# Warm-up products, key products in column tiles, a later exponential and finer transfers in a linear-attention and expert kernel

## The chip, the cores and the metric

The kernel runs on one core of a Trainium2 chip. The metric is the device time of one execution in microseconds (us). A core has TensorE (PE, with its weight loads shown apart as PEld), VectorE (DVE), ScalarE (ACT), GpSimd (POOL) and SyncE (SP, which here issues nearly all transfers). They run on their own instruction queues, each in order, and meet through semaphores.

## The reference

Two stages, in float32. Attention: 4 batches, 8 heads, 576 tokens, width 64. A feature map projects q and k by one 64x128 matrix, subtracts the largest absolute value of each row, and takes the exponential of both signs:

```python
proj = np.einsum('bhsd,df->bhsf', x, w_phi)
proj = proj - np.max(np.abs(proj), axis=-1, keepdims=True)
return np.concatenate([np.exp(proj), np.exp(-proj)], axis=-1)
...
kv = np.einsum('bhsf,bhsd->bhfd', k_p, v);  z = np.sum(k_p, axis=2)
num = np.einsum('bhsf,bhfd->bhsd', q_p, kv)
den = np.einsum('bhsf,bhf->bhs', q_p, z)[..., None] + 1e-06
```

Then a mixture of 8 experts over the 2304 tokens (512 wide): argmax of the gate's logits picks one expert, each expert takes the first 576 tokens that chose it, and computes `relu(x @ w1) @ w2` (512 to 1024 to 512), scaled by the gate's weight.

## The kernel before

The tokens are taken in two halves of 1152 (p = 0, 1), each of 9 blocks of 128 rows; heads go in two groups of four (g = 0, 1). An item is one block of one head group: 18 key items, then 18 query items for each half, 72 in all. A loop over t (L673) issues the items as a software pipeline: in step t stand the projection of item t, the maximum and subtraction of item t-1 (`center`, L263), the exponentials or transposes of item t-2, the products with kv of query item t-3, and the sums of key item t-4 (`kv_sum`, L328). The order of instructions on each engine is the order in which this loop writes them.

- **Projection** (`project`, L246). The first seven key blocks multiply raw float32 columns (L254). All others use a float16 split: `x_split` (L189) makes on ACT the rounded half and on POOL the remainder (L194, L195), and eight products of 128x128 by the two float16 parts of the matrix follow (L259, L260).
- **Sums of keys** (L342). Each item has 16 products of 64 columns of weights, alternating between the lower and the upper half of the output partitions, each as two passes.
- **Gates.** `vgate` puts the gate's logits of the values beside them (L219, L229, L241).
- **Routes.** `route` (L415) queues small steps for a group of blocks in `pending`; `tick()` works them off in between DVE's instructions of `center`. For the first group (9 blocks) ACT takes the exponential `es` right after the one-hot rows `oh` (L481), then DVE reduces `oh` (L536), then `swaps` finds the fullest expert and POOL reorders the experts (L488 to L496), and `sel` reads the reordered offsets `perm["s"]` (L539). The logits `lt` that `es` reads and the results of L536 lie in one PSUM tile, `sm_t`.
- **Transfers.** All wait in SP's queue. `paced` lets a transfer wait for the latest subtraction of `center`. Empty rows are written to `xs` by 18 fills of 256 rows (L157), paced, at t from 18 to 47. `x_load` (L180) brings a tile of q or k whole, not paced, eight steps ahead of its split; the second half's `v` and `vT` come in four transfers at t = 19 and 23. Scatters of rows (L459) begin at t = 56.

`warm` (L278) issues products of the identity into the PSUM tile `pt`; nothing calls it. After the attention the experts' products follow (L814 to L848), weights loaded per expert.

Of the kernel before, what the change touches and what calls it, by code (L numbers as in the profile page):

```python
# [20 lines left out]
P = 128  # L21
# [11 lines left out]
XW = DM + 2  # L33
# [4 lines left out]
def tile_kernel(ctx: ExitStack, tc: tile.TileContext, qT, kT, vT, vv, w_phi, w_g, w1, w2, out, cap):  # L38
# [110 lines left out]
    def paced(dma):  # L149
        tc.add_manual_dep(dma.ins, beat[0].ins.name, mybir.DependencyInfo(  # L150
            mybir.DependencyClass.Sync, mybir.DependencyReason.DATA), reason="pace")

    def fill_xs(i, n):
        r0, r1 = (NE * slots * j // n for j in (i, i + 1))
        nr = (r1 - r0) // P
        if nr:
            paced(nc.sync.dma_start(xs[r0:r0 + nr * P, :].rearrange("(r p) c -> p r c", p=P),  # L157
                                    fill.unsqueeze(1).to_broadcast([P, nr, XW])))
        if r1 - r0 - nr * P:
            nc.sync.dma_start(xs[r0 + nr * P:r1, :], fill[0:r1 - r0 - nr * P])  # L160

    tokf = cpool.tile([P, NT // P], F32, tag="tokf", name="tokf")
    nc.gpsimd.iota(tokf, pattern=[[P, NT // P]], base=SKIP, channel_multiplier=1,
# [16 lines left out]
    def x_load(kind, p, g, c, cut=0):  # L180
        c0, c1 = runs[c]
        if (kind, p, g, c) not in raw_x:
            raw_x[kind, p, g, c] = px_p.tile([P, 2, c1 - c0], F32, tag=f"px{c}", name="px")
        lo, hi = (0, cut) if cut > 0 else (-cut, c1 - c0)
        src = (kT if kind == "k" else qT)[2 * g:2 * g + 2, :, p * TP + c0 + lo:p * TP + c0 + hi]
        nc.sync.dma_start(raw_x[kind, p, g, c][:, :, lo:hi], src.rearrange("i d c -> d i c"))


    def x_split(kind, p, g, c, odd):  # L189
# [58 lines left out]
    def project(kind, p, g, r):  # L248
        pr = ps_p.tile([P, 4, NF], F32, tag="pr", name="pr")
        c = int(r > MIX)  # L250
        cols = slice(r * P - runs[c][0], (r + 1) * P - runs[c][0])
        if (kind, p, g) == ("k", 0, 0) and r < 7:
            for i in range(2):
                nc.tensor.matmul(pr[:, 2 * i:2 * i + 2], raw_x[kind, p, g, c][:, i, cols], wpair,  # L254
                                 start=True, stop=True)
        else:
            for j in range(4):
                lt = stk[kind, p, g, c, j % 2][:, j // 2, cols]
                nc.tensor.matmul(pr[:, j], lt, whi, start=True, stop=False)  # L259
                nc.tensor.matmul(pr[:, j], lt, wlo, start=False, stop=True)  # L260
        return pr

    def center(pr):  # L263
# [151 lines left out]
    def route(blk, n, xr, lg):  # L415
# [106 lines left out]
        def ready():  # L522
# [9 lines left out]
            lambda: v.scalar_tensor_tensor(ef, lt, 0.0, io, ALU.is_ge, ALU.mult),  # L532
            lambda: v.tensor_reduce(flat(ix), ef, AX.X, ALU.min),
            lambda: v.tensor_tensor(oh, ix.to_broadcast([P, n, NE]), io, ALU.is_equal),
            *([number, exps] if late else [exps] if old is None else []),
            lambda: v.tensor_reduce(rn[:, 0], oh.rearrange("p n e -> p e n"), AX.X, ALU.add),  # L536
            run_total,
            *([*swaps(), rest, rest, rest] if old is None else []),
            lambda: v.tensor_tensor(sel, oh, perm["s"].unsqueeze(1).to_broadcast([P, n, NE]), ALU.mult),  # L539
            lambda: v.tensor_reduce(flat(sl), sel, AX.X, ALU.add),  # L540
            positions,
            *([] if late or old is None else [exps, rest, rest, rest]),
# [77 lines left out]
    def attention():  # L620
# [4 lines left out]
        def plan(c, marks):  # L625
            ends = []
            for x, split in zip([(K, 0, 0)][:c] + [(K, 0, 1), (Q, 0, 0), (Q, 0, 1), (K, 1, 0), (K, 1, 1), (Q, 1, 0), (Q, 1, 1)], marks):
                for odd in range(2):
                    at.setdefault(split[odd], []).append((*x, c, odd))
                ends.append(max(split))  # L630
                if x[:2] != (K, 0):
                    free = ends[-4] if len(ends) > 3 else 6
                    load_at.setdefault(max(free + 2, min(split) - 8), []).append((*x, c))

        plan(0, [(5, 6), (12, 13), (15, 16), (25, 26), (31, 32), (42, 44), (46, 49)])
        plan(1, [(3, 4), (10, 11), (19, 21), (23, 24), (28, 29), (37, 39), (55, 51), (57, 53)])
# [11 lines left out]
        x_load(K, 0, 1, 1)  # L648
        v_load(0, MIX + 1, NBLK, 1)
        rests = []  # L650

        def bank(i):
            def f():
# [8 lines left out]
            for i, f in enumerate(parts):  # L662
                early.setdefault(t + min(i, 3 - t) if t == 2 else t + i, []).append(f)

        FILLS = [*range(18, 36, 3), *range(36, 48)]
        OPEN = 56
        depth = 4
        for t in range(len(items) + depth):
            for i, lag in ((0, 0), (2, 2), (3, 3), (6, 4), (1, 1), (4, 4), (7, 5)):
                n = t - lag  # L670
                if 0 <= n < len(items) and items[n].get(i):
                    items[n][i]()
            for f in early.get(t, []):  # L673
                f()
            for f in rests:
                f()
            calm[0] = 0 if t < 36 or len(swapped) > 1 else 2 if t in (46, 49) else 1
            for x in load_at.get(t, []):
                x_load(*x)
            rests = [x_split(*x) for x in at.get(t, [])]  # L680
            if scatters and t >= OPEN:
                scatters.popleft()()
            if t >= len(items):
                for _ in range(4):
                    if pending:
                        step()
            if t in FILLS:
                for i in range(len(FILLS)):
                    if FILLS[i] == t:
                        fill_xs(i, len(FILLS))  # L690
            if t in (19, 23):
                vt_load(1, 0, NBLK, (t - 19) // 4)
                v_load(1, 0, NBLK, (t - 19) // 4)
            if t == 54:
                assert swapped
                for e in range(NE):
                    who[e] = nc.values_load(perm_i[0:1, e:e + 1], engines=[mybir.EngineType.SP], min_val=0,
                                            max_val=NE - 1)
            if 56 <= t < 72 and t % 2 == 0:
                half = (t - 56) // 2  # L700
                paced(w_load(0, half // 2, half % 2 * 2, half % 2 * 2 + 2))
            if t == 60:
                rctx.close()
                first_p.append(ctx.enter_context(tc.tile_pool(name="first_p", bufs=1, side="right")))
                for c in range(2):
                    w_t[c] = w_pair(first_p[0], c)
                x2_l.append(first_p[0].tile([P, 4, 2, slots], F32R, tag="xh", name="xh"))
                for s0, _ in tiles[:2]:
                    xi_t[0, s0] = first_p[0].tile([P, XW], F32, tag=f"xi{s0}", name="xi")
            if t == 67:  # L710
                assert len(row_dmas) >= NBLK
                load_x(0, 0, 2, row_dmas[:NBLK])
            if 64 <= t < 72:
                w_lo(*divmod(t - 64, 4), nc.gpsimd)
            if 63 <= t < 71:
                w_hi(*divmod(t - 63, 4))
            if t == 68:
                who["seen"] = nc.values_load(seen_i[0:1, 0:1], engines=engines, min_val=0, max_val=NT)
                tc.mark_branch_hint_location("seen", hint=who["seen"] > wide - 1, engines=engines[:3])
            if t in (72, 73):  # L720
                prep(0, *tiles[t - 72], ps_p.tile([P, 4, NF], F32, tag="pr", name="pr"))
# [392 lines left out]
```

## Time and profile before

| | us |
|---|---|
| median of three runs | 427.6 (426.96 to 427.92) |
| profiled execution | 425.98 |
| its span, first to last instruction | 424.2 |
| PE busy / weight loads / DVE / ACT / POOL | 405.1 / 357.7 / 265.9 / 245.9 / 175.4 |
| DMA mean | 195 GB/s |

The profiled execution takes 425.98 us: the span of 424.2 us and 1.8 us around it. The attention runs to about 164 us, the experts from there to the end. Busy time of PE counts a product until its modelled end, so a full slice is not an engine at its peak. In the chain of waits, "issue" is time for which the profile shows no cause.

### The profile page before, as it was taken

What the parts mean: (1) busy time and instruction counts of PE and PEld (TensorE: products, weight loads), DVE (VectorE), ACT (ScalarE), POOL (GpSimd) and SP (SyncE); (2) the same over time, 40 slices, a digit from 0 to 9 for tenths busy, and PEclk for the clock granted to TensorE, in tenths of its full rate; (3) what the DMA queues carried; (4) which work ended last, traced back from release to release, by engine and by line L of the source; (5) the groups of instructions that cost most, each with busy time, mean ns of one, the idle gap of its engine ahead of it and who ended that gap; (6) DMA issues with size and microseconds to landing.
All of it is one profiled execution on the core that took longest, in us unless ns stands there. A gap on an engine that the chain in (4) does not pass through costs nothing.

```text
span 424.2 us, 12166 instructions
## 1 busy us (share of the span) xinstructions
PE 405.1 (95%) x4813; PEld 357.7 (84%) x4813; DVE 265.9 (63%) x585; ACT 245.9 (58%) x452; POOL 175.4 (41%) x215
## 2 busy tenths in 40 slices
PE   6999999999799989999999999999999999999992
PEld 4788888888789878989979898989898998799871
DVE  5776898887788797833247975757475464156410
ACT  3978687779776766712146855656565454155410
POOL 1848566448576778730035306042241500160011
PEclk9999999999899999999999999999999999999997
DMA  7990599489506743479007995977959176210010
GB/s 254 388 353 5 170 328 372 138 287 307 172 6 222 227 171 107 175 249 368 5 32 223 341 338 192 331 226 224 324 179 349 64 240 228 93 36 0 2 51 29
DMA packets 42715, 82.78 MB, mean 195 GB/s; under 512 B 4351, under 2 KB 9343, under 8 KB 42624
## 3 DMA queue, kind: packets, MB, share of 16 engines
q1 hardware_dynamic: 38080, 72.13, 50.5%
q0 software_dynamic: 4544, 9.47, 6.2%
q8 instruction: 53, 0.87, 0.9%
q14 instruction: 38, 0.31, 0.2%
HBM read 62.65 MB, written 24.30 MB: 205 GB/s over the span
## 4 chain that ended last, share of the span: by engine, by line
PE 83%; POOL 4%; issue 4%; ACT 4%; DVE 3%; DMA 1%; POOLq 0%; ACTq 0%
PE ph L814 9%; PE ph L815 9%; PE ph L817 9%; PE acc L342 8%; PE acc L371 5%; PE sm L847 4%; PE sm L845 4%; PE sm L848 4%; PE ph L845 4%; PE ph L847 4%; PE ph L848 4%; PE pr L259 3%; PE pr L260 2%; PE pr L254 2%; PE pt L747 2%
## 5 line engine op out<-in xcount | busy, mean ns | idle before, releaser
L169 POOL DMA_INDIRECT out<-y,it x22 | 24.4, 1111 | 164.4 <-ACT y L860 86.7
L123 DVE TENSOR_TENSOR l<-raw,h 128x512 fp32r<-128x512 f32 x118 | 79.6, 706 | 19.6 <-ACT h L117 16.9
L195 POOL TENSOR_TENSOR stk<-px,stk 64x1024 f16<-64x1024 f32 (+1 forms) x30 | 70.8, 2363 | 38.6 <-ACT stk L194 37.7
L814 PE MATMUL ph<-xh,h 128*128 128x256 f32 (+3 forms) x292 | 79.4, 298 | 0.1
L815 PE MATMUL ph<-xh,l 128*128 128x256 f32 (+3 forms) x292 | 78.9, 296 | 0.0
L117 ACT ACTIVATE h<-raw 128x512 fp32r<-128x512 f32 x128 | 75.7, 629 | 0.0
L828 ACT ACTIVATE h<-ph 128x256 fp32r<-128x256 f32 (+3 forms) x67 | 28.8, 429 | 53.6 <-PE ph L817 52.9
L831 DVE SCALAR_TENSOR_TENSOR h<-ph,h 128x256 fp32r<-128x256 f32 (+2 forms) x91 | 33.3, 388 | 39.2 <-ACT h L828 38.8
L814 PEld LDWEIGHTS ph<-xh,h 128*128 128x128 f32 x292 | 55.6, 191 | 1.2 <-issue 0.2
L815 PEld LDWEIGHTS ph<-xh,l 128*128 128x128 f32 x292 | 55.7, 191 | 0.9
L265 DVE TENSOR_REDUCE m<-pr 128x4 f32<-128x512 f32 x72 | 49.2, 684 | 8.6 <-PE pr L260 5.1
L269 DVE TENSOR_TENSOR d<-pr,m 128x512 f32<-128x512 f32 x72 | 49.7, 691 | 4.0 <-ACT kp L316 0.4
L817 PE MATMUL ph<-xh,h 128*128 128x256 f32 (+3 forms) x292 | 50.9, 296 | 0.0
L342 PE MATMUL acc<-v,kp 128*64 128x73 f32 (+1 forms) x1280 | 46.3, 231 | 1.1 <-issue 1.1
L342 PEld LDWEIGHTS acc<-v,kp 128*64 128x64 f32 (+1 forms) x1280 | 40.7, 138 | 5.8 <-issue 2.6
L371 PE MATMUL acc<-kv,qp 128*64 128x73 f32 x1152 | 44.5, 229 | 0.0
L371 PEld LDWEIGHTS acc<-kv,qp 128*64 128x64 f32 x1152 | 39.1, 136 | 6.0 <-issue 5.7
L817 PEld LDWEIGHTS ph<-xh,h 128*128 128x128 f32 x292 | 42.7, 191 | 0.6
L259 PE MATMUL pr<-whi,stk 128*128 128x128 f16 x260 | 36.9, 223 | 2.6 <-DVE d L269 2.3
L260 PE MATMUL pr<-wlo,stk 128*128 128x128 f16 x260 | 36.4, 221 | 0.0
L194 ACT ACTIVATE stk<-px 64x1024 f16<-64x1024 f32 (+1 forms) x30 | 34.5, 1150 | 0.5
L358 ACT ACTIVATE qp<-pt 128x512 f32<-128x512 f32 x36 | 21.5, 596 | 21.1 <-PE pt L356 21.0
(163 smaller groups left out, 715.8 us busy)
## 6 DMA issues: line engine op xcount, KB each, us to landing
raw<-in_w SPq DMA_DIRECT2D x28, 1024.0 KB, 7.9
xs<-fill SPq DMA_DIRECT2D x18, 514.0 KB, 6.1
xr<-xs SPq DMA_DIRECT2D x24, 257.0 KB, 7.9
raw<-in_w SPq DMA_DIRECT2D x8, 512.0 KB, 4.3
vt<-in_vT SPq DMA_DIRECT2D x3, 1152.0 KB, 12.7
v<-in_vv SPq DMA_DIRECT2D x2, 1314.0 KB, 11.9
px<-in_kT SPq DMA_DIRECT2D x5, 512.0 KB, 8.5
px<-in_qT SPq DMA_DIRECT2D x4, 640.0 KB, 9.3
```

The lines of the kernel that those rows point to most:

```text
L117: nc.scalar.activation(hi, a, AF.Copy)
L123: engine.tensor_tensor(lo, a, hi.bitcast(F32), ALU.subtract)
L195: return lambda: nc.gpsimd.tensor_tensor(t[other], x, t[own], ALU.subtract)
L259: nc.tensor.matmul(pr[:, j], lt, whi, start=True, stop=False)
L260: nc.tensor.matmul(pr[:, j], lt, wlo, start=False, stop=True)
L265: nc.vector.tensor_reduce(m.rearrange("p a b -> p (a b)"), pr, AX.X, ALU.max, apply_absolute_value=True)
L269: beat[0] = nc.vector.tensor_tensor(d, pr, m.to_broadcast([P, 4, NF]), ALU.subtract)
L342: nc.tensor.matmul(acc[f:f + D, a, j * GC:(j + 1) * GC], kp[lo:hi, j, a, f:f + D], vt[lo:hi, r, h * GC:(h + 1) * GC], start=first and j == ...
L371: nc.tensor.matmul(num[lo:hi, g, j * GC:(j + 1) * GC], qp[:, a, j, lo:hi], kv_t[b][:, a, 4 * g + j], start=(a == 0), stop=(a == 1))
L814: nc.tensor.matmul(acc, hi[:, k, fs], xh[:, k, o:o2], start=(k == 0), stop=False)
L815: nc.tensor.matmul(acc, lo[:, k, fs], xh[:, k, o:o2], start=False, stop=False)
L817: nc.tensor.matmul(acc, hi[:, k, fs], xl[:, k, o:o2], start=False, stop=(k == 3))
```

## The change

1. Six products of the identity (128x128) are issued on PE ahead of everything else.
2. In the projection of keys (all of the first half that use the split, and blocks 0 to 3 of head group 0 of the second half) each 128x128 product becomes two of 64 weight columns, written to the lower and the upper half of the partitions, both with the first float16 part and then both with the second.
3. In the first route group the exponential moves behind the swap; a copy of `perm["s"]` into `sm_t` is added, and every group's `sel` reads that copy.
4. 36 fills of 128 rows instead of 18 of 256, at t from 19 to 53.
5. Tiles of q and k come in two halves at two steps, paced, and start 7 steps ahead of the split (4 for the first half's queries); `v` and `vT` of the second half come in twelve transfers at t = 19 to 30.

```diff
+        dma = nc.sync.dma_start(raw_x[kind, p, g, c][:, :, lo:hi], src.rearrange("i d c -> d i c"))
+        if beat[0] is not None:
+            paced(dma)
...
                 lt = stk[kind, p, g, c, j % 2][:, j // 2, cols]
-                nc.tensor.matmul(pr[:, j], lt, whi, start=True, stop=False)
-                nc.tensor.matmul(pr[:, j], lt, wlo, start=False, stop=True)
+                if kind == "q" or p and (g or r >= 4):
+                    nc.tensor.matmul(pr[:, j], lt, whi, start=True, stop=False)
+                    nc.tensor.matmul(pr[:, j], lt, wlo, start=False, stop=True)
+                    continue
+                for w in (whi, wlo):
+                    for o in range(0, P, D):
+                        nc.tensor.matmul(pr[o:o + D, j], lt[:, o:o + D], w, start=w is whi, stop=w is wlo,
+                                         skip_group_check=True)
...
-            *([number, exps] if late else [exps] if old is None else []),
+            *([number, exps] if late else []),
             lambda: v.tensor_reduce(rn[:, 0], oh.rearrange("p n e -> p e n"), AX.X, ALU.add),
             run_total,
-            *([*swaps(), rest, rest, rest] if old is None else []),
-            lambda: v.tensor_tensor(sel, oh, perm["s"].unsqueeze(1).to_broadcast([P, n, NE]), ALU.mult),
+            *([*swaps(), exps, rest, rest, rest, lambda: v.tensor_copy(sm_t[:, TOT:TOT + NE], perm["s"])]
+              if old is None else []),
+            lambda: v.tensor_tensor(sel, oh, sm_t[:, TOT:TOT + NE].unsqueeze(1).to_broadcast([P, n, NE]), ALU.mult),
...
-                    load_at.setdefault(max(free + 2, min(split) - 8), []).append((*x, c))
+                    first = max(free + 2, min(split) - (4 if x[:2] == (Q, 0) else 7))
+                    for i in range(2):
+                        load_at.setdefault(first + i, []).append((*x, c, (1 - 2 * i) * (runs[c][1] - runs[c][0]) // 2))
...
+        warm(6)
...
-        FILLS = [*range(18, 36, 3), *range(36, 48)]
+        FILLS = [*range(19, 36, 2), *range(36, 54), *range(37, 54, 2)]
...
-            if t in (19, 23):
-                vt_load(1, 0, NBLK, (t - 19) // 4)
-                v_load(1, 0, NBLK, (t - 19) // 4)
+            if 19 <= t < 31:
+                (vt_load if t % 2 else v_load)(1, (t - 19) // 2 % 3 * 3, (t - 19) // 2 % 3 * 3 + 3, (t - 19) // 6)
```

The order of instructions at three places. On ACT, in the keys of the second half, where the first route group's exponential `es` stands before (`kp` are the keys' exponentials, two an item; `stk` are splits):

```order
L194 ACTIVATE stk<-px 64x1280
L315 ACTIVATE kp<-d 128x4x128
L316 ACTIVATE kp<-d 128x4x128
L481 ACTIVATE es<-sm 128x72
L315 ACTIVATE kp<-d 128x4x128
```

and at the same place on ACT in the changed kernel, as far as the moved `es`:

```order
L190 ACTIVATE stk<-px 64x1280
L317 ACTIVATE kp<-d 128x4x128
L318 ACTIVATE kp<-d 128x4x128
L317 ACTIVATE kp<-d 128x4x128
L318 ACTIVATE kp<-d 128x4x128
L317 ACTIVATE kp<-d 128x4x128
L318 ACTIVATE kp<-d 128x4x128
L190 ACTIVATE stk<-px 64x1280
L317 ACTIVATE kp<-d 128x4x128
L318 ACTIVATE kp<-d 128x4x128
L317 ACTIVATE kp<-d 128x4x128
L318 ACTIVATE kp<-d 128x4x128
L483 ACTIVATE es<-sm 128x72
```

`es` goes four items down ACT's queue. On DVE the reduction of `oh` (L536 before, L538 after) keeps its place; the new copy (L540 after) stands three pairs of `center` behind the last step of the swap on DVE, and `sel` one instruction of `center` behind the copy.

On PE, the last products of one key item's projection and the sums behind it, before:

```order
L259 LDWEIGHTS stk
L259 MATMUL pr<-whi,stk 128x128
L260 LDWEIGHTS stk
L260 MATMUL pr<-wlo,stk 128x128
L342 MATMUL acc<-v,kp 64x73 x16
```

and in the changed kernel, the last of its four heads:

```order
L261 LDWEIGHTS stk
L261 MATMUL pr<-whi,stk 64x128
L261 LDWEIGHTS stk
L261 MATMUL pr<-whi,stk 64x128
L261 LDWEIGHTS stk
L261 MATMUL pr<-wlo,stk 64x128
L261 LDWEIGHTS stk
L261 MATMUL pr<-wlo,stk 64x128
L344 MATMUL acc<-v,kp 64x73 x16
```

Two products and two weight loads of a head have become four of each, and the projection now has the sums' shape of 64 weight columns.

At the start of PE's queue, before (raw projections of the first items, gate, sums):

```order
L254 MATMUL pr<-wpair,px 128x256 x6
L219 MATMUL pt<-vt,gwp 32x128 x8
L254 MATMUL pr<-wpair,px 128x256 x2
L229 MATMUL pt<-ident,vg 128x128
L254 MATMUL pr<-wpair,px 128x256 x2
```

and in the changed kernel:

```order
L283 MATMUL pt<-ident 128x128 x6
L250 MATMUL pr<-wpair,px 128x256 x6
L215 MATMUL pt<-vt,gwp 32x128 x8
L250 MATMUL pr<-wpair,px 128x256 x2
L225 MATMUL pt<-ident,vg 128x128
```

The six products stand ahead of the first item; the rest follows in the same order.

## Rows read from the trace of the kernel before

**Rows 1.** The page: busy time by engine; the chain that ended last, by engine

```profile
PE 405.1 (95%) x4813; PEld 357.7 (84%) x4813; DVE 265.9 (63%) x585; ACT 245.9 (58%) x452; POOL 175.4 (41%) x215
...
PE 83%; POOL 4%; issue 4%; ACT 4%; DVE 3%; DMA 1%; POOLq 0%; ACTq 0%
```

**Rows 2.** Windows: us, busy us of each engine (instructions), granted clock, DMA share, GB/s

```profile
23.00:42.40 19.40, 18.32 (x442) 15.71 (x435) 13.70 (x29) 16.07 (x24) 12.93 (x6) 1.00 0.43 161
...
90.00:104.80 14.80, 14.54 (x363) 12.96 (x361) 13.09 (x28) 14.68 (x24) 12.40 (x9) 1.00 0.93 308
...
104.80:112.00 7.20, 4.87 (x81) 4.37 (x80) 3.87 (x8) 5.97 (x10) 3.41 (x2) 0.76 0.93 315
...
164.00:424.00 260.00, 251.57 (x1584) 225.11 (x1584) 136.51 (x288) 123.14 (x255) 71.30 (x134) 0.99 0.53 177
```

**Rows 3.** Timeline of the start: start us, us, engine, line, tiles [idle before]

```profile
1.20 0.29 POOL L52 TENSOR_SCALAR_AFFINE_SELECT ident<-ident 128x128 f32<-128x128 f32 x1
...
4.12 1.36 PEld L254 LDWEIGHTS pr<-wpair,px 128*128 128x128 f32 x4 [4.12 <-DVE gwp L89]
...
6.96 0.69 DVE L269 TENSOR_TENSOR d<-pr,m 128x512 f32<-128x512 f32 x1
...
7.77 1.43 PEld L254 LDWEIGHTS pr<-wpair,px 128*128 128x128 f32 x4 [0.27 <-issue]
...
10.23 0.73 PEld L254 LDWEIGHTS pr<-wpair,px 128*128 128x128 f32 x4 [0.20 <-issue]
```

**Rows 4.** Transfers of the key tiles in the first 10 us: issue to landing

```profile
DMA to landing us min/median/max: 2.3/7.1/14.0
```

**Rows 5.** Timeline, POOL and PE: the splits before the tenth key block

```profile
16.66 5.31 POOL L195 TENSOR_TENSOR stk<-px,stk 64x1280 f16<-64x1280 f32 x2 [0.19 <-ACT stk L194]
...
23.02 0.23 PE L259 MATMUL pr<-whi,stk 128*128 128x128 f16 x1
```

**Rows 6.** Chain in order of time, one key block: start, us, what

```profile
44.24 0.16 PE pr L259
...
44.40 0.06 PE pr L260
...
44.80 1.18 PE acc L342 x32
```

**Rows 7.** Lines by form, 42 to 46 us, weight loads: busy us, mean ns

```profile
L342 PEld LDWEIGHTS acc<-v,kp 128*64 128x64 f32 x64 | 2.2, 136 | 0.2
...
L260 PEld LDWEIGHTS <-stk 128*128 128x128 f16 x9 | 0.9, 98 | 0.0
```

**Rows 8.** Chain in order of time: one of two pauses inside the sums

```profile
26.47 0.64 issue
```

**Rows 9.** Timelines of DVE, ACT and PE around 105 us

```profile
103.28 0.68 DVE L265 TENSOR_REDUCE m<-pr 128x4 f32<-128x512 f32 x1
...
107.46 0.29 DVE L536 TENSOR_REDUCE sm<-oh 128x8 f32<-128x72 bf16 x1 [3.50 <-ACT es L481]
...
107.22 0.21 ACT L481 ACTIVATE es<-sm 128x72 f32<-128x72 f32 x1
...
104.82 1.25 PE L342 MATMUL acc<-v,kp 128*64 128x73 f32 x32
...
109.36 2.21 PE L342 MATMUL acc<-v,kp 128*64 128x73 f32 x32
...
112.18 1.25 PE L342 MATMUL acc<-v,kp 128*64 128x73 f32 x32
```

**Rows 10.** Timelines of POOL and DVE: the swap and its first reader

```profile
117.59 0.24 POOL L494 TENSOR_SCALAR perms<-perme 128x8 f32<-128x8 f32 x1
...
119.83 0.59 DVE L539 TENSOR_TENSOR sel<-oh,perms 128x72 f32<-128x72 bf16 x1
```

**Rows 11.** Timelines of SP and POOL: last fills, first scatter

```profile
101.33 7.41 SPq L157 DMA_DIRECT2D xs<-fill  x3
...
128.16 1.24 POOL L459 DMA_INDIRECT xs<-xr,si  x1 [2.31 <-DVE d L269]
```

More of the change, by code (lines that the diff above doesn't have):

```diff
@@ L151, in paced, with fill_xs @@
             mybir.DependencyClass.Sync, mybir.DependencyReason.DATA), reason="pace")
[L153 to L160, printed above, removed]
+    def fill_xs(r0, r1):
+        paced(nc.sync.dma_start(xs[r0:r1, :], fill[0:r1 - r0]))
     tokf = cpool.tile([P, NT // P], F32, tag="tokf", name="tokf")
@@ L185, in x_load @@
         src = (kT if kind == "k" else qT)[2 * g:2 * g + 2, :, p * TP + c0 + lo:p * TP + c0 + hi]
-        nc.sync.dma_start(raw_x[kind, p, g, c][:, :, lo:hi], src.rearrange("i d c -> d i c"))
+        dma = nc.sync.dma_start(raw_x[kind, p, g, c][:, :, lo:hi], src.rearrange("i d c -> d i c"))
+        if beat[0] is not None:
+            paced(dma)
     def x_split(kind, p, g, c, odd):
@@ L663, in attention @@
                 early.setdefault(t + min(i, 3 - t) if t == 2 else t + i, []).append(f)
-        FILLS = [*range(18, 36, 3), *range(36, 48)]
+        FILLS = [*range(19, 36, 2), *range(36, 54), *range(37, 54, 2)]
+        filled = [0]
         OPEN = 56
@@ L686, in attention @@
                         step()
[L687 to L690, printed above, removed]
-            if t in (19, 23):
-                vt_load(1, 0, NBLK, (t - 19) // 4)
-                v_load(1, 0, NBLK, (t - 19) // 4)
+            for _ in range(FILLS.count(t)):
+                fill_xs(filled[0], min(filled[0] + P, NE * slots))
+                filled[0] += P
+            if 19 <= t < 31:
+                (vt_load if t % 2 else v_load)(1, (t - 19) // 2 % 3 * 3, (t - 19) // 2 % 3 * 3 + 3, (t - 19) // 6)
             if t == 54:
-                assert swapped
+                assert swapped and filled[0] >= NE * slots
                 for e in range(NE):
```

## The prediction

> **What bounds the kernel now.** I read the page's busy times and its chain first [rows 1]: PE is busy 95% of the span and holds 83% of the chain, and no other engine has over 4% of it. So a microsecond is worth something where it is taken from PE, or from whatever PE waits for. [...] The expert stage, 164 to 424 us, has PE busy 251.6 of 260 us; the change does not touch it, and its loads are issued relative to PE's progress, so an earlier start of that stage arrives whole at the end. From 23 to 42.4 us PE is busy 18.32 of 19.40 us, with ACT close behind at 16.07.
>
> **Part 1, six products of the identity.** [...] The identity is ready at 1.20 + 0.29 = 1.49 us [rows 3]; six float32 products are twelve passes. A raw pass of 256 columns at the low level takes 1.43 / 4 = 0.36 us or a little more; one of 128 columns about 0.2, so the six end near 1.6 + 12 x 0.2 = 4.0 us. The first key tile is issued at 1.74 us and lands 2.3 us later at the earliest [rows 4], about 4.0: the products fit before it, and delay the first item by 0 to 0.3 us. If the clock then rises 2.5 us earlier (about 7 instead of 9.5), the third and fourth items run at the high level and save about 0.6 us each. What is late next is DVE: the third item waits for a buffer that the first subtraction frees (6.96 + 0.69 = 7.65, the item starts at 7.77 [rows 3]). Working the chain PE, maximum, subtraction on to the fifth item I get 0.9 to 1.1 us. There is a second cap: the tenth key block needs two remainders that POOL ends at 16.66 + 5.31 = 21.97 us, and its first product starts at 23.02 [rows 5]. POOL's splits hang on ACT and on landings, not on PE, so no more than about 1.0 us of everything before can pass that point. I take 1.0; ends: 0.3 lost, 1.2 won.
>
> **Part 2, column tiles.** One key block costs PE 0.56 + 1.18 = 1.74 us [rows 6]. Inside the projection a product takes 0.06 us, but the first takes 0.16: 0.10 us goes where PE turns from 64-column tiles back to full width. The sums' 32 weight loads come every (1.10 - 0.136) / 31 = 31 ns (64 loads are 2.2 us busy [rows 7]), so 32 passes are 0.99 us and the other 0.19 of the 1.18 is the turn the other way. Projection and sums in one shape leave out up to 0.29 us; I take 0.25, because some of the first pair's wait for weights remains. The new projection has 16 loads and 16 products for 8 and 8. The sums show what two half-width tiles cost: a pair with its two loads every 62 ns, against 60 ns for one full-width product [rows 6, 7]. Eight pairs are then 0.50 us against 0.45, within the 0.04 I held back. So 0.25 us a block.
>
> In the first half eleven blocks change. Two lie before the POOL cap, and their gain is inside Part 1's 1.0. Nine lie between 23 and 42.4 us: 9 x 0.25 = 2.25 us. In this stretch there are two pauses inside the sums, one of 0.64 us that the profile can only call "issue" [rows 8]; the query loads stand in the same time and now come later and in halves, so I count 0.4 us of it back. PE's 19.40 us would become 16.75, and ACT has 16.07 us of work there [rows 2]: it becomes the next bound, nearly at once. For its queueing I take off 0.4 and write 2.2 us for the stretch. The four blocks of the second half alternate with query work that is full width, so each keeps one turn; and from 90 to 104.8 us ACT is busy 14.68 of 14.80 [rows 2]. I take 0.3 us for all four (ends: 0 and 1.0).
>
> [...] The rows show a 64-column float32 load sustained at 31 ns and a full-width float16 load of 98 ns hidden behind products 60 ns apart [rows 6, 7]. [...]
>
> **Part 3, the exponential.** At 103.28 + 0.60 us DVE is free and sits 3.50 us idle until 107.46, because L536 writes the tile that `es` reads on ACT; `es` runs at 107.22, behind a split and two exponentials of keys, as the order on ACT shows [rows 9]. Behind L536 stands the next subtraction, and behind that PE's projection: the sums start at 104.82, then 109.36 (2.21 us long at the low level instead of 1.25) and 112.18 [rows 9]. [...] Without the wait the two sums would stand at the cadence of 1.74: 104.82 + 1.74 = 106.56 and 108.30. The second stands at 112.18, so 3.9 us are lost. ACT must then have the exponentials of those items: it has them by about 107.3, since it only loses the 0.2 us of `es`. What is late next is the swap: POOL delivers `perm["s"]` at 117.83 and DVE reads it at 119.83 [rows 10], 2.0 us of slack. POOL's part hangs on a split on ACT that comes only about 1.4 us earlier, DVE comes 3.9 earlier; the slack goes to about 0 and the new copy may wait 0 to 1 us, with the next `center` queued behind it. `es` itself ends four items earlier than the copy needs it. I take 3.7 us; ends 1.0 and 4.0. The copy costs DVE some 0.15 us once, hidden in its waits for PE, and `sel` out of `sm_t` may take less than the 0.59 us of [rows 10]; both at nothing.
>
> **Parts 4 and 5, transfers.** Bytes are the same. Fills end six steps later; now SP issues the last ones between 101.33 and 108.74 and the first scatter, which needs them all, starts at 128.16 [rows 11]. Six key items of 1.74 us leave 19.4 - 10.4 = 9.0 us for the last landing; loads of the busy first 10 us took 7.1 at the median [rows 4]. No cost, a reserve of about 2 us. Split tiles arrive three steps or more ahead of use. Cost 0; ends 0.3 won and 1.5 lost (a split that waits on ACT in front of exponentials).
>
> **Sum.** 1.0 + 2.2 + 0.3 + 3.7 = 7.2 us from the profiled execution: 425.98 - 7.2 = 418.8. The three timed runs lie 1.0 to 1.9 us above it, their median 1.6; so 427.6 - 7.2 = 420.4 us.
>
> **Rivals.**
> A, the early gains end at ACT and POOL: for it, ACT's 16.07 of 19.40 [rows 2] and the cap [rows 5]; against it, ACT sits idle in that stretch for 3 us. Only Part 3 and 0.3 count: 427.6 - 4.0 = 423.6.
> B, the wait moves to the copy: POOL is late by 3 us, DVE stalls there as before. For it the slack of 2.0, against it POOL's short chain. 427.6 - 7.2 + 3 = 423.4.
> C, the warm-up does nothing: the clock rises when it did, the first item is 0.2 late. The cap then takes the two blocks' 0.5 only: 427.6 - 6.6 = 421.0.
> D, half-width float16 loads set the pace at 60 ns each, as a full-width product does now: 16 x 0.06 = 0.96 for 0.70 (0.45 and the turns), 0.26 lost instead of 0.25 won, on 15 blocks 3.9 us; Parts 1 and 3 give 4.7 less the cap's lost share 0.5: 427.6 - 4.2 + 3.9 = 427.3, no change. [...]
> E, the slower side: each of the 16 products waits for its own load because two loads no longer pass a product. At 98 to 136 ns [rows 7] that is 1.57 to 2.18 us a block for 0.70, 0.87 to 1.48 lost on 15 blocks: 427.6 - 4.2 + 13 = 436, up to 446. It decides from 0.28 us a block, some 61 ns a product. Against it, the sums do the very same with float32 weights at 31 ns.
>
> **How the numbers follow.** Forecast 0.58 (its own range 418.0 to 422.5), C 0.09, A 0.11, B 0.09, D 0.07, E 0.06. Low end: every part at its better end is 1.2 + 2.9 + 1.0 + 4.0 + 0.3 = 9.4, 418.2, and 0.7 for the spread of runs: 417.5. High end 425.5 takes in A, B and C; D, E and the tails are outside. Differences under 0.2% (0.9 us) can't be told from none: same 0.06 from D, slower 0.06 from E, the rest faster, 0.88.
>
> **What would show it.** Right: PE's loads at 0.73 us for four by about 7 us; L261 products in pairs 60 ns apart and a block at 1.5 us; no wait of DVE on ACT at L538 and a clock of 1.00 from 104 to 112; the expert stage as long as before, some 7 us earlier. Wrong: L261 products one by one at 60 ns or more; a wait of DVE for POOL at L540; a clock that still rises at 9 to 10 us; ACT without idle time from 22 to 40 us while PE waits.

## The result and the profile after

| | before, us | changed, us | ratio (95%) |
|---|---|---|---|
| first comparison, medians of 6 and 6 runs | 427.28 | 420.93 (420.33 to 421.7) | 0.9866 (0.983 to 0.990) |
| the same kernel in a later batch of runs, 35 and 12 runs | 427.6 | 426.66 (425.61 to 428.34) | 0.9971 (0.995 to 1.000) |
| profiled executions of the first comparison | 425.98 | 421.7 | |

The forecast was 420.4, and the first comparison gave 420.93. The second line belongs beside it: in a later batch, on chip 13, the same program kept only 0.9 of the 6.4 us (on which chip the first comparison ran is not on record, so chip and batch can't be told apart), and the last experiment below shows where in the program 4.2 us of it went. Where executions of a variant fell into a slower state of the chip (four of twelve with the exponential early again, one of twelve in the first run with column tiles only later), its time below is the median of the others. In the two profiles the first expert product comes at 167.97 us before and at 163.52 after, 4.45 us earlier, and the expert stage is as long as it was (256.2 and 256.4).

The page of the changed kernel, which answers to [rows 1]:

```profile
PE 405.7 (97%) x4945; PEld 359.0 (85%) x4945; DVE 263.4 (63%) x586; ACT 245.3 (58%) x452; POOL 175.5 (42%) x215
...
PE 91%; DVE 3%; POOL 2%; issue 1%; ACT 1%; POOLq 0%; DVEq 0%; ACTq 0%
```

Its windows, against [rows 2] (length, then busy us and count of PE, PEld, DVE, ACT and POOL, the granted clock, the DMA share and GB/s):

```profile
23.00:42.40 19.40, 17.60 (x484) 15.72 (x481) 13.16 (x28) 15.39 (x23) 12.87 (x6) 0.91 0.33 99
...
90.00:104.80 14.80, 14.66 (x375) 13.05 (x375) 13.27 (x29) 14.47 (x24) 11.84 (x9) 1.00 0.86 249
104.80:112.00 7.20, 7.20 (x172) 6.38 (x169) 6.15 (x14) 7.15 (x12) 4.67 (x3) 1.00 1.05 343
```

From 104.8 to 112 PE is now busy throughout at a clock of 1.00: that pause is gone. From 23 to 42.4 us, where the column tiles were to gain most, the clock is 0.91 and PE's busy time is lower than before: it stands more. The weight loads of the start, against [rows 3]; the first line is of before, the second four loads there:

```profile
6.14 1.36 PEld L254 LDWEIGHTS pr<-wpair,px 128*128 128x128 f32 x4 [0.66 <-DMA px<-in_kT]
...
1.53 2.63 PEld L283 LDWEIGHTS pt<-ident 128*128 128x128 f32 x12 [1.53 <-POOL ident L52]
4.16 1.35 PEld L250 LDWEIGHTS pr<-wpair,px 128*128 128x128 f32 x4
5.99 0.73 PEld L250 LDWEIGHTS pr<-wpair,px 128*128 128x128 f32 x4 [0.48 <-DMA px<-in_kT]
```

The second four loads take 0.73 us, not 1.36, and the trace's record of the granted clock begins, with 1.00 of full speed, at 5.9 us instead of 9.4; this is meant below where the clock "rises". Ahead of it the trace has no record: that the clock is low there is read from the loads. What the prediction calls the low level stands in the records as 0.50 (before, 108.4 to 111.8 us: 32 products of the sums take 2.21 us), the high one as 1.00 (1.25 us) [rows 9].

What the tiles did to one block, and PE's products from 22.5 us on. The first two lines are of before, where a projection starts and where the next one does; the others are of the changed kernel, beginning with the same two places:

```profile
19.56 0.22 PE L259 MATMUL pr<-whi,stk 128*128 128x128 f16 x1
...
21.28 0.23 PE L259 MATMUL pr<-whi,stk 128*128 128x128 f16 x1
...
18.75 0.25 PE L261 MATMUL pr<-whi,stk 128*64 128x128 f16 x2
...
20.25 0.22 PE L261 MATMUL pr<-whi,stk 128*64 128x128 f16 x2
...
22.57 1.06 PE L344 MATMUL acc<-v,kp 128*64 128x73 f32 x27
25.44 0.22 PE L344 MATMUL acc<-v,kp 128*64 128x73 f32 x1 [1.80 <-issue]
25.59 0.64 PE L215 MATMUL pt<-vt,gwp 128*32 128x128 f32 x16
...
26.36 0.30 PE L261 MATMUL pr<-wlo,stk 128*64 128x128 f16 x2
26.45 0.32 PE L261 MATMUL pr<-whi,stk 128*64 128x128 f16 x2
26.55 0.32 PE L261 MATMUL pr<-wlo,stk 128*64 128x128 f16 x2
```

The block takes 1.50 us for 1.72. But inside one block's sums PE stands for 1.80 us with no releaser. Just behind, the pairs of column tiles go from 0.055 us apart to 0.10: the granted clock is 0.50 from 26.4 to 29.8 us. Nothing of this stands before; its "issue" pause was 0.64 us [rows 8].

The first route group on DVE and ACT, against [rows 9]:

```profile
103.49 0.63 ACT L317 ACTIVATE kp<-d 128x512 f32<-128x512 f32 x1
...
104.57 0.29 DVE L538 TENSOR_REDUCE sm<-oh 128x8 f32<-128x72 bf16 x1
104.90 0.17 DVE L478 CAST rb<-sm 128x8 bf16<-128x8 f32 x1
104.98 0.68 DVE L271 TENSOR_TENSOR d<-pr,m 128x512 f32<-128x512 f32 x1
...
116.19 0.24 POOL L496 TENSOR_SCALAR perms<-perme 128x8 f32<-128x8 f32 x1
...
116.47 0.17 DVE L540 COPY sm<-perms 128x8 f32<-128x8 f32 x1
```

L538 starts without a wait (it waited 3.50 us), and the copy L540 follows POOL's last step at once, without a stall of its own.

One difference was not in the forecast. It is at the second route group, and needs rows of before that were not shown: DVE, POOL and PE, first before, then after.

```profile
148.94 1.01 POOL L459 DMA_INDIRECT xs<-xr,si  x1 [0.17 <-issue]
149.50 3.04 DVE L539 TENSOR_TENSOR sel<-oh,perms 128x32 f32<-128x32 bf16 x1
149.98 2.49 POOL L123 TENSOR_TENSOR l<-raw,h 128x512 fp32r<-128x512 f32 x2
...
152.82 0.18 PE L455 MATMUL sm<-oh,tri 128*128 128x32 bf16 x1 [1.78 <-DVE sm L540]
```

```profile
146.29 1.01 POOL L461 DMA_INDIRECT xs<-xr,si  x1 [0.17 <-issue]
146.85 0.18 DVE L542 TENSOR_TENSOR sel<-oh,sm 128x32 f32<-128x32 bf16 x1
...
147.33 2.51 POOL L123 TENSOR_TENSOR l<-raw,h 128x512 fp32r<-128x512 f32 x2
...
148.32 0.19 PE L457 MATMUL sm<-oh,tri 128*128 128x32 bf16 x1
```

The same multiplication of 32 elements a partition took 3.04 us where it read `perm["s"]` in SBUF, and 0.18 where it reads the copy in PSUM. Both times it began 0.56 us into POOL's scatter (L459, L461). That scatter alone does not hold it: the same line with both inputs in SBUF took 0.17 us beside the same scatter at another group of before, where no L123 followed.

```profile
171.88 0.17 DVE L539 TENSOR_TENSOR sel<-oh,perms 128x16 f32<-128x16 bf16 x1
```

At 149.50 it ended 0.07 us behind POOL's two L123 (149.98 + 2.49 = 152.47), and PE waited 1.78 us for it.

When each item's subtraction starts (DVE L269 before, L271 after) places the gains. Before minus after, us:

```
item      7     8     9    20    32    45    46    66    67    71   first expert product
gain   +0.9  +1.0  -0.8  +0.3   0.0  -0.6  +2.7  +2.6  +5.5  +4.5  +4.5
```

So: start +0.9, the stretch of the tiles -0.6 by item 20, -0.3 and -0.5 more up to item 45, the exponential +3.2, `sel` +2.9, and -1.1 behind it. About half of this last loss is a small operation of the same group, `drop` (L549 before, L552 after): it took 0.16 us before and 0.63 now, ending 0.04 us behind one of POOL's L123.

### The profile page after: what moved, and what is told of

The parts are those of the page before. It is cut to its first block, busy times and chain, and to the rows that moved or that the text cites. A ratio compares the mean times of both kernels' runs of the same rounds, so it can differ in the third digit from the quotient of the medians.

```text
span 419.9 us, 12502 instructions
## 1 busy us (share of the span) xinstructions
PE 405.7 (97%) x4945; PEld 359.0 (85%) x4945; DVE 263.4 (63%) x586; ACT 245.3 (58%) x452; POOL 175.5 (42%) x215
## 4 chain that ended last, share of the span: by engine, by line
PE 91%; DVE 3%; POOL 2%; issue 1%; ACT 1%; POOLq 0%; DVEq 0%; ACTq 0%
PE ph L819 9%; PE ph L820 9%; PE ph L822 9%; PE acc L373 9%; PE acc L344 9%; PE sm L852 4%; PE sm L850 4%; PE sm L853 4%; PE ph L850 4%; PE ph L852 4%; PE ph L853 4%; PE pt L358 3%; PE pr L256 3%; PE pr L257 2%; PE pt L752 2%; POOL stk L191 2%
## 5 line engine op out<-in xcount | busy, mean ns | idle before, releaser
L123 DVE TENSOR_TENSOR l<-raw,h 128x512 fp32r<-128x512 f32 x118 | 79.6, 705 | 19.6 <-ACT h L117 16.8
L271 DVE TENSOR_TENSOR d<-pr,m 128x512 f32<-128x512 f32 x72 | 49.7, 690 | 4.1 <-ACT kp L318 0.4
L850 PE MATMUL sm<-h,h 128*128 128x512 f32 x72 | 29.0, 403 | 0.4 <-issue 0.4
L256 PE MATMUL pr<-whi,stk 128*128 128x128 f16 x200 | 28.2, 221 | 0.4 <-POOL stk L191 0.2
```

The source lines that it names most:

```text
L123: engine.tensor_tensor(lo, a, hi.bitcast(F32), ALU.subtract)
L271: beat[0] = nc.vector.tensor_tensor(d, pr, m.to_broadcast([P, 4, NF]), ALU.subtract)
L850: nc.tensor.matmul(py[0:m], h_t[f][:, s0:s0 + m], hi, start=(f == 0), stop=False, skip_group_check=True)
```

## The experiments

Three batches, each on one chip (1, 7 and 13) and with its own runs of before: the first (426.48 us for before) takes one edit out at a time, the second (427.68) adds or moves, the third (427.6) repeats what the second left in doubt beside the unaltered changed kernel. Only the third holds the changed kernel itself. What the first two say of it crosses batches in the medians, and is therefore read from the steps between items in the profiles.

**Without column tiles** (batch 1)

```diff
-                if kind == "q" or p and (g or r >= 4):
+                if True:
```

> The changed kernel with every split projection at full width again (no column tiles). Theory 1: in the first half the tiles' gain of 0.25 us a block is real, but it goes into the pause of PE at the next 256 instructions of its program (2.0 us at 25.4 us, and half clock behind it), so leaving the tiles out costs little: 0 to 0.7 us slower, 421 to 421.7, a block back at 1.74 us and the pause near 0.9 us with no half-clock stretch there. Rival: the tiles carry the 2.2 us that the prediction gave them, and without them it is 423.

Measured 421.22 us, ratio 0.9887 (0.985 to 0.992): as fast as with them in the first comparison. In its profile the pause near 25 us is 1.08 us for 1.80, and the clock stays at 1.00 from 5.3 to 411.5 us; item 20 is 1.3 us earlier than with the tiles, the first expert product 1.9.

```profile
25.76 0.22 PE L257 MATMUL pr<-wlo,stk 128*128 128x128 f16 x1 [1.08 <-issue]
```

As placed here, the tiles gain nothing net.

**`sel` reads SBUF again** (batch 1)

```diff
-lambda: v.tensor_copy(sm_t[:, TOT:TOT + NE], perm["s"])
-v.tensor_tensor(sel, oh, sm_t[:, TOT:TOT + NE].unsqueeze(1)...
+v.tensor_tensor(sel, oh, perm["s"].unsqueeze(1)...
```

> The changed kernel in which the product by the offsets (sel) reads the small tile on SBUF again and the copy into PSUM is left out. Theory 1: that read, beside POOL's work, was the 3.04 us instruction of DVE at 149.5 us of the kernel before, and comes back with 1.8 us or more of the time: 422.5 to 424. Rival: its place in time was chance and it takes 0.2 to 0.6 us wherever it falls now: 421.

Measured 425.24 us, ratio 0.9967 (0.995 to 0.999), above the range of the first theory, and 4.0 above the kernel without tiles in the same batch, which differs from it by the tiles as well (of the 5.5 us between these two profiles at the first expert product, 2.9 lie in the step from item 66 to 67). That step takes 4.87 us again (2.00 with the copy). Its rows repeat those of before:

```profile
147.25 3.04 DVE L542 TENSOR_TENSOR sel<-oh,perms 128x32 f32<-128x32 bf16 x1
147.73 2.50 POOL L123 TENSOR_TENSOR l<-raw,h 128x512 fp32r<-128x512 f32 x2
...
150.57 0.18 PE L457 MATMUL sm<-oh,tri 128*128 128x32 bf16 x1 [1.77 <-DVE sm L543]
...
152.44 2.06 PE L373 MATMUL acc<-kv,qp 128*64 128x73 f32 x32
```

The last row shows what follows PE's wait: 32 products in 2.06 us at the low clock (1.24 at the high one). That the read of `perm["s"]` in SBUF costs this step 2.9 us is shown.

**The exponential early again** (batch 1)

```diff
-*([number, exps] if late else []),
+*([number, exps] if late else [exps] if old is None else []),
...
-*([*swaps(), exps, rest,
+*([*swaps(), rest,
```

> The changed kernel with the first route group's exponential back in front of the reduction of the one-hot rows. Theory 1: DVE waits about 3.5 us for ACT again and the time is 3.3 to 3.7 us longer, 424.3 to 424.7. Rival: with all else changed ACT is less far behind there, the wait is 1 us or less and the time 421 to 422.

Measured 425.35 us, ratio 0.9998 (0.996 to 1.004). DVE's wait at L538 is back:

```profile
107.07 0.29 DVE L538 TENSOR_REDUCE sm<-oh 128x8 f32<-128x72 bf16 x1 [2.76 <-ACT es L483]
```

Item 45 to 46 takes 4.99 us (1.74 in the changed kernel): 3.2 us for Part 3, of which 2.1 are left at item 49; the clock does not fall behind this wait, as it did before (108.4 to 111.8 us). In total it loses 4.1 us to the kernel without tiles, and 5.7 in the two profiles; 2.4 of these lie in its expert stage (258.6 us), which I did not follow.

This profile also shows that the six products do not always bring the early clock. The first projection starts at 5.06 us here (4.25 in the changed kernel), after PE has stood 0.60 us for the first key tile, and the clock rises at 10.0 us, as late as without the products.

**Without the six products** (batch 1)

```diff
-        warm(6)
```

> The changed kernel without the six products of the identity. Theory 1: the clock rises some 2.5 to 3.5 us later, the first blocks are 0.9 us late and it stays so to the end: 421.8. Rival: the 0.9 us ends at POOL's splits or at the pause at 25 us, which hangs on the transfer of the program's code: 421.0, no change.

Measured 425.17 us, ratio 0.9981 (0.995 to 1.001). The start is 2.0 us later (item 4 at 15.37 for 13.39 us), twice the forecast: 0.8 of it is the first key tile, which landed later here (first projection at 5.07 for 4.25 us), and about 1.2 are left for the clock, which rises at 10.8 us for 5.9. But by item 9 that is made up, since the later PE does not pause near 25 us at all, by item 13 it is 1.4 us ahead, and the first expert product comes at 163.95. On the way PE waits for POOL's split:

```profile
43.77 0.23 PE L256 MATMUL pr<-whi,stk 128*128 128x128 f16 x1 [1.05 <-POOL stk L191]
```

Five profiles with the tiles have this wait, 0.95 to 1.05 us (this one, `sel` in SBUF, the early exponential, and the six products at item 43 or in both places), and the lead of each over the changed kernel shrinks by 0.8 us from item 13 to item 21. The loss is in the expert stage, 261.5 us long, where PE stands twice with no releaser:

```profile
222.48 0.40 PE L821 MATMUL ph<-xh,h 128*128 128x256 f32 x2 [1.03 <-issue]
...
229.10 0.35 PE L798 MATMUL ph<-xh,l 128*128 128x128 f32 x1 [1.42 <-issue]
```

The clock then falls to its low level from 229.3 to 232.7 us. None of this is work that the six products touch.

**Before plus the copy for `sel` alone** (batch 2)

```diff
-lambda: v.tensor_tensor(sel, oh, perm["s"].unsqueeze(1)...
+lambda: v.tensor_copy(sm_t[:, TOT:TOT + NE], perm["s"])
+lambda: v.tensor_tensor(sel, oh, sm_t[:, TOT:TOT + NE].unsqueeze(1)...
```

> The kernel before with one thing changed: the permutation's row is copied into sm_t behind the swaps, and the multiplication to sel reads that copy in PSUM. Theory 1 (from the run without the copy, where the step from item 66 to item 67 took 4.87 us again against 2.01): sel at the second routing costs 0.2 us in place of 3.04, the products behind it wait less, and the time falls by 2 to 3.5 us, to 423 to 424.5 beside 426.5 for before. Rival 1 (the gain needs the faster first half, since it only decides whether sel falls into the scatter on POOL): no change, 426 to 427. Rival 2 (the copy waits for the permutation and stands in VectorE's way at the first routing): 0.5 to 1 us of the gain is lost at item 46 to 49.

Measured 432.7 us, ratio 1.0126 (1.011 to 1.015): slower, against all three expectations. The step from item 66 to 67 did fall to 2.01 us. But some steps on, another small operation of the same group met POOL:

```profile
154.88 2.52 POOL L123 TENSOR_TENSOR l<-raw,h 128x512 fp32r<-128x512 f32 x2
...
155.58 5.29 DVE L550 TENSOR_SCALAR drop<-pr 128x4 f32<-128x4 f32 x1
...
157.36 1.04 POOL L412 TENSOR_TENSOR xr<-nb,rd 128x512 f32<-128x512 f32 x1
...
158.36 2.47 POOL L123 TENSOR_TENSOR l<-raw,h 128x512 fp32r<-128x512 f32 x2
...
161.51 0.22 PE L259 MATMUL pr<-whi,stk 128*128 128x128 f16 x1 [3.12 <-DVE d L269]
```

Four elements a partition took 5.29 us: L550 ended at 160.87, 0.04 behind the last of POOL's five operations in a row (158.36 + 2.47 = 160.83). In eleven other profiles the same operation takes 0.43 to 0.96 us and ends 0.03 to 0.04 us behind one of POOL's L123, for 0.16 in the two where POOL was idle. The rest of the 5.0 us is only in part in this profile, which is of the fastest of the six runs: it goes from 1.8 us ahead of before at item 60 to 0.5 behind at item 66, where completions come late as in the last experiment below. So the gain at `sel` is not a property of the copy alone: a few us earlier or later, the next small operation falls beside POOL.

**The transfers of before** (batch 2, and again in 3): fills, loads of q, k, v and vT in the old sizes and places.

```diff
-        FILLS = [*range(19, 36, 2), *range(36, 54), *range(37, 54, 2)]
+        FILLS = [*range(18, 36, 3), *range(36, 48)]
...
-                    for i in range(2):
-                        load_at.setdefault(first + i, []).append(...)
+                    load_at.setdefault(max(free + 2, min(split) - 8), []).append((*x, c))
```

> The changed kernel with the transfers of before: fills, loads of x and of v and vT in the old sizes and at the old places. Theory 1 (forecast: transfers are worth nothing either way): within 0.7 us of the changed kernel, 420.3 to 421.7. Rival 1 (the unpaced halves of the loads crowd the start and the code of TensorE): the pause near 25 us goes or moves, and the first half is 1 to 2 us shorter or longer. Rival 2 (the fills in smaller pieces took the place of the gain): the second half's stretch from item 19 to 36 changes by over 1 us.

> The variant with the transfers of before once more, beside the changed kernel itself. Theory 1 (the transfers decide where TensorE's and ScalarE's next instructions arrive late): 3 us or more above the changed kernel of this job, with a pause of TensorE of about 2 us near 26 us and one of over 1 us near 78 us, and ScalarE's 2.5 us near 138 us. Rival (the transfers are worth nothing, and the 427.4 was that job's): within 1 us of the changed kernel of this job.

Measured 427.38 us in batch 2, which did not hold the changed kernel, and 427.34 in batch 3 beside 426.66: 0.7 us, with intervals that overlap. The rival of the second text holds; transfers are worth nearly nothing, as forecast, though the pauses of its first theory are there: one of 1.23 us, which ends at 76.97 us, brings the profile from 0.3 to 1.8 us behind the unaltered kernel at item 33, and 1.3 are left at the first expert product.

**The six products at item 43** (batch 2)

```diff
-        warm(6)
...
+            if t == 43:
+                warm(6)
```

> The changed kernel with the six products of the identity at item 43, in the stretch bound by ScalarE, in place of the program's start: the same number of TensorE instructions in all, without the early clock. Theory 1 (the four us between the changed kernel and the one without the products, of which the first stage shows none by item 12, come from the place of the later instructions in the program's code, whose pauses in the expert stage differ): 421 to 422, and the expert stage 256 to 257 us. Rival (the early clock is worth them, by whatever way): 424.5 to 425.5, as without the products. Rival 2 (the products in their new place cost time themselves): item 44 or 45 is over 1 us later.

Measured 425.98 us, ratio 0.9964 (0.995 to 0.998), the expert stage 257.2 us. Its number lies in no range of the three texts, and its expert stage is near the first theory's. The second rival held: item 44 comes 2.80 us behind item 43, for 1.50 in the changed kernel. The time can't be read against the 421 of the first comparison, because the unaltered kernel stood at 426.66 in batch 3; beside that, in another batch, the place of the six products makes no difference that these runs can tell.

**Column tiles only later** (batch 2, and again in 3): not in blocks 7 and 8 of group 0 and block 0 of group 1.

```diff
-                if kind == "q" or p and (g or r >= 4):
+                if kind == "q" or not p and (not g or r < 1) or p and (g or r >= 4):
```

> The changed kernel with column tiles only from the second block of the second group of the first half on, and in the second half's four blocks: the three blocks before, where TensorE stood for 2.03 us and its clock then fell, go back to full-width products. Theory 1 (the tiles run TensorE ahead of its code while the transfers fill the DMA engines; later, with the engines free, they gain their 0.25 us a block): no pause over 1 us near 25 us, item 20 0.8 to 1.5 us earlier than in the changed kernel, the time 419.5 to 420.5. Rival (the tiles' gain ends at ScalarE or POOL wherever it is): item 20 within 0.4 us, the time 421 to 421.5.

> The variant with the first three blocks of column tiles taken back, once more beside the changed kernel. In its profile it was 2.3 us ahead of the changed kernel at item 20 and 1.5 us ahead at item 46, and lost it behind. Theory 1 (the loss belongs to it: its later instructions fall on other places of the program's code): 426 or above again. Rival (the loss was that job's): 419.5 to 420.5, and the best kernel of the case.

Measured 428.34 and 429.25 us, the latter 2.6 above the unaltered kernel of its batch. The tiles do gain there: item 20 is 2.2 us and the first expert product 1.7 us earlier than in the unaltered kernel of batch 3 (45.70 against 47.92, 164.74 against 166.43). From item 4 to item 20 the two profiles take 32.0 and 31.9 us, the kernel without tiles 33.3, the changed kernel 34.3. So eight tiled blocks gain 1.3 us net where no stretch at the low clock follows; 0.25 a block would be 2.0. Then the expert stage takes 262.7 us against 257.7, in both batches with pauses before the same instructions:

```profile
242.03 0.28 PE L820 MATMUL ph<-xh,l 128*128 128x256 f32 x1 [1.96 <-issue]
```

What these pauses have in common can be read from the transfers. The page of each profile lists a DMA queue of instructions, q8, with packets of 16 KB; in this document they are called code packets. In all 14 profiles, PE has 19 pauses of 0.6 us or more between 20 and 410 us for which the profile gives "issue"; here are eight:

```
kernel, PE resumes at      last code packet starts, takes   from its end to PE, us
before           27.11     24.75  1.09                      1.27
changed          25.44     22.93  1.09                      1.42
changed, again   25.68     23.20  1.10                      1.38
no six products  222.48    219.89 1.16                      1.43
no six products  229.10    226.77 0.93                      1.40
old transfers    76.97     74.63  0.94                      1.40
tiles later      25.91     23.37  1.11                      1.42
tiles later      242.03    239.59 1.11                      1.33
```

Eighteen of the 19 end 1.27 to 1.48 us after the packet's end (the other 1.71), while such a packet comes only every 8 us in the mean. Those near 25 us stand at the same place of PE's recorded instructions, the 705th or 706th, and before's next pause of the kind (0.43 us) 256 later. I read this as PE waiting for its own program; no experiment changed when the code comes. Near 25 us the DMA engines were full while the packet moved (a share of 0.95 from 22.9 to 24.1 us in the changed kernel), but not ahead of 222 us (0.21), and the packet's own 1.09 us are the usual ones (median 1.08). Why it does not start earlier the trace does not show.

**Twelve products in all** (batch 3): six at the start and six at item 43.

```diff
+            if t == 43:
+                warm(6)
```

> The changed kernel with six more identity products at item 43, in the stretch bound by ScalarE: the work behind it is unchanged, but every later TensorE instruction stands 24 places later in the program's code. Theory 1 (the place of the code alone moves the time by several us, since it decides which products stand first behind a stretch of code that has not arrived): up to item 43 as the changed kernel, then pauses with no releaser at other instructions, and 2 us or more away from it in the total, 423 to 426. Rival (the place does not matter): within 0.7 us of the changed kernel of this job.

Measured 426.58 us beside 426.66: the rival holds. Here too item 44 comes 2.80 us behind item 43, so the products cost 1.3 us there, which a lead of 1.1 us over the unaltered kernel nearly makes up in its profile. Moving the later code by 24 instructions did not move the total out of the rival's 0.7 us.

**The changed kernel again** (batch 3)

> The changed kernel once more, unaltered, in one job with three variants, since the last three variants came out 4 to 7 us above its first time in a job that did not hold it, with waits in their first halves that none of the earlier traces has (ScalarE idle 2.5 us at its 224th recorded operation, TensorE's pauses at its 705th and 3010th instruction). Theory 1 (those times belong to the variants): 420.5 to 421.5 as in its first job. Rival (they belong to the conditions of that job, and the changed kernel would have shown them too): in a job where the two variants repeated below stay at 427 to 428.5, it is at 424 or above.

Measured 426.66 us: the rival holds; the times of batch 2 belonged to conditions that batch 3 shares. The profile repeats the first one within 0.25 us up to item 45 (pause at 25.7 us included), and is then 0.8 behind by item 49, 2.8 by item 67 and 2.9 by the first expert product; 1.3 more go in the expert stage. At item 61, DVE, PE and ACT, here and then in the first profile of the same kernel:

```profile
133.99 0.60 PE L358 MATMUL pt<-ident,d 128*128 128x128 f32 x4
...
134.62 0.17 DVE L394 TENSOR_SCALAR rd<-acc 128x8 f32<-128x8 f32 x1 [1.17 <-PE pt L358]
...
136.15 0.60 ACT L360 ACTIVATE qp<-pt 128x512 f32<-128x512 f32 x1 [2.53 <-remote]
```

```profile
133.32 0.17 DVE L394 TENSOR_SCALAR rd<-acc 128x8 f32<-128x8 f32 x1 [0.20 <-PE acc L373]
...
133.66 0.60 PE L358 MATMUL pt<-ident,d 128*128 128x128 f32 x4
...
134.30 0.60 ACT L360 ACTIVATE qp<-pt 128x512 f32<-128x512 f32 x1 [1.01 <-PE pt L358]
```

PE's transposes are put 0.33 us later than in the first profile, the exponential that needs them 1.85 us. As far as the semaphores are recorded (these profiles lack 3 to 10 records that the others have), products' completions come 0.5 to 1.6 us behind their modelled ends at 9 or more places, nearly all from about 130 us on, in all eight profiles of batches 2 and 3; in the six of before, the changed kernel and batch 1 there is at most one such case, of 0.57 us. The granted clock is 1.00 from 120 to 165 us in both profiles of the changed kernel, and the DMA engines are no busier (a share of 0.64 from 128 to 150 us, 0.68 in the first). Why completions are late there, the trace does not show, and no run here asks. Nor is there a profile of before under those conditions; its median is 0.3 to 1.2 us higher there.

## Why the prediction was right, and where it was not

- **Part 1, the start**: forecast 1.0 us, measured 0.9, so rival C is out in that comparison. The 1.0 rests on a clock that rises at about 7 instead of 9.5 us, my estimate; no run shows that the rise follows PE's first work by a fixed time: it is 5.3 us in the kernel before (4.12 to 9.4) and 4.4 in the changed kernel (1.53 to 5.9). With the products at the start the clock rises at 4.6 to 7.4 us in nine of ten profiles, and without them at 8.5 to 10.8 in four; but in the tenth, with the early exponential, it rises at 10.0, as rival C had it. What the six products are worth at the end stays open: 4 us in batch 1, by pauses 200 us later, nothing between batches 2 and 3.
- **Part 2, the column tiles**: the step that failed. A block did shrink as worked out: from the start of a projection to the next it took 1.50 us (18.75 to 20.25) for 1.72 (19.56 to 21.28), and D and E are out. But "ACT becomes the next bound" was wrong near 25 us: the first bound was, as I read the times of the code packets, the arrival of PE's own code. A quicker PE gets to that place sooner, stands 1.80 us (1.08 without tiles), and pays again with 3.4 us at the low clock (1.3 us by item 13 against the run with `sel` in SBUF, which has the same pause and kept its clock; 0.7 by item 20, 0.1 by item 33). Rival A's mechanism is there too, behind it: in five profiles whose clock did not fall there, PE waits about 1 us for POOL's split near 43.5 us. I had the 0.64 us pause in front of me [rows 8], called it an unexplained "issue" and counted 0.4 us of it back. Of 2.2 us, -0.6 remained by item 20. The four blocks of the second half were to give 0.3; items 36 to 38 lost 0.4.
- **Part 3, the exponential**: forecast 3.7, measured 3.2 in the profiles and 3.2 by taking it back, of which 2.1 last there. No wait moved to the copy, so rival B is out. One reading was off without touching the sum: DVE is free at 103.28 + 0.68 = 103.96 us, not + 0.60.
- **`sel` in PSUM**, costed "at nothing": 2.9 us in the profiles, both by putting the copy in and by leaving it out. I looked at the first `sel` only [rows 10], 0.59 us with a slack of 2 us, and not at the same line at the second group, where 3.04 us stood on PE's path.
- **Parts 4 and 5, transfers**: 0, measured 0.7 at most.

In the profiles the parts make 0.9 - 0.6 - 0.3 - 0.5 + 3.2 + 2.9 - 1.1 = 4.5 us, with rounding the 4.45 above, for a forecast of 7.2; the medians of that comparison differ by 6.35, and the 1.9 us more stand in no profile. So the number was met by luck: two errors of opposite sign, about 4 us too much for the tiles and 3 too little for `sel`, and a difference of medians larger than that of the profiles. The second measurement, 426.66, lies outside the range: I had taken the spread of the runs at 0.7 us, and late completions of PE were no case of mine.

On `sel` the traces show this: 3.04 us twice beside POOL with both inputs in SBUF, 0.18 with one input in PSUM. It began 0.48 us before POOL's first L123, during a scatter that elsewhere did not hold it (0.17 us at 171.88), and was held until the second L123 had ended. What of POOL's work held it, and whether the same held L550 for 5.29 us, no run shows.

## What to carry to other kernels

A short operation whose time is many times that of its twin (here 3.04 us for 0.18) may be held, not at work: list every instance of a line by duration, and for VectorE look at what GpSimd does beside it. An "issue" pause of TensorE may be its program arriving: look for a code packet that ends 1.3 to 1.5 us ahead of its end (18 of 19 here). Work that made TensorE quicker there and doubled its instructions made that pause longer (1.80 us for 1.08). And a gain of 1.3% in one batch of runs may be 0.3% in another: measure again in a second batch before believing small parts of it.

## What the runs showed of the hardware

- TensorE's pauses of 0.6 us or more without a releaser end 1.27 to 1.48 us after a 16 KB code packet in 18 of 19 cases. Behind four of the five pauses of 1.8 to 2.0 us near 25 us, the granted clock was 0.50 for 3.4 us.
- VectorE operations of 4 and 32 elements a partition were held 5.29 and 3.04 us beside runs of GpSimd instructions and ended 0.04 to 0.07 us behind the last of them, without being let in between. That is not always so: `sel` at 119.83 us [rows 10] ended 0.09 us behind the first of two GpSimd splits.
- 64-column tiles in float16: pairs 0.055 to 0.056 us apart at a granted clock of 1.00, two loads and two products each, the same as for one full-width product with its load (0.05 to 0.06 us apart in the kernel before, from 19.56 to 19.95).
- The same program had TensorE's completions 0.5 to 1.6 us late in batch 3 (chip 13), as its variants had in batch 2 (chip 7), and on time in the first comparison; left open.
